# Batch 1 of a fused block-sparse attention and Swish MLP kernel: x transposes by DMA, odd value rows by ScalarE, pair 3's key maxima at another time, one copy for the last half tile, and a table load at another place

## The chip, the cores and the metric

The kernel runs on one core of a Trainium2 chip. The time is the device time in microseconds of one execution; the kernel before was run three times. A profile of one further execution gives, for each instruction, when it started and ended and what it waited for.

Engine names as in the profile: PE is TensorE (matmuls; PEld are its weight loads), DVE is VectorE, ACT is ScalarE, POOL is GpSimd, SP is SyncE. DMAs are issued from the queues of SP, ACT and POOL.

## The reference

```python
# q, k, v: (4, 8, 768, 64); block 32, window 16
k_sum = k.reshape(B, H, nb, block, D).max(axis=3)
v_sum = v.reshape(B, H, nb, block, D).mean(axis=3)
scores_l = scale * q @ k^T,  kept where |i - j| < window
scores_s = scale * q @ k_sum^T + log(block)
a = softmax over [scores_l, scores_s];   out = a @ [v, v_sum]
x = out, heads joined: (3072, 512)
h = x @ w_in                             # w_in (512, 2048)
g = h * sigmoid(beta * h)
result = g @ w_out                       # (3072, 512) float32
```

## The kernel before

**Tiling.** Four batches go one after the other; within a batch the eight heads go in four pairs (pair 0 to 3), each pair 128 wide, and the 768 positions in six tiles of 128. Attention gives x of a pair with positions in the partitions (`x_nat`); the first matmul needs it the other way round, so each pair is transposed into one quarter of `xT`. The MLP then makes `h` from all four quarters (`h_group`, L488: matmuls with `ki` 0 to 3, one for each pair, then Silu on ScalarE into `h_sb`), and the output tiles from `h_sb` (`o_part`, L512: 16 matmuls to a tile of 128 positions, in four parts, a copy out of PSUM, a DMA). The reciprocal of beta is folded into `w_out`.

**Local scores.** A score block sets 64 queries against a key row of 96 window keys, with the 24 block maxima behind them. Queries 0 to 63 of a tile use the even rows (`kw[:, 0]`, `ve`), queries 64 to 127 the odd rows (`kw[:, 1]`, `vo`), which are the same data 64 positions on. For a batch after the first:

- `cross` (L300) turns k and q of a pair by DMA transposes from SP's queue; `prep_k` and `prep_q` do it on PE, for pairs 0 and 1 of batch 1.
- `top_k` (L291, one DVE reduce) or `max_k` takes the block maxima; `rows_k` (L315, two DVE copies, L319 and L320) writes odd rows and maxima into `kw`.
- `copy_v` (L322) copies the odd rows `vo` from `ve`, two pieces to a pair, by DMA from SP's queue unless another way is handed in; `mean_v` and `rows_v` (L349, two DVE copies) add the block means behind each row, in `ve` and in `vo`.
- `scores` (L427) makes the scores of one half on PE and takes Exp on ScalarE; `mask` (L440) multiplies by the band on DVE; `av` (L444) multiplies with `ve` and `vo` on PE; `norm` (L459) divides on DVE into `x_nat`; `x_transpose` (L468) turns it: by six PE transposes with an identity and a DVE copy (L479, L480) in batches 0 and 1, by one DMA transpose on SP's queue (L474) in batches 2 and 3.

**PSUM.** A ring `big` of three buffers holds scores, av, `px` and h; a ring `t` of two holds the output tiles, so output tile n waits until tile n - 2 is copied out.

**Order.** Each engine runs its instructions in the order in which the program gives them; nothing is reordered. The main loop (L629 on) builds that order for one batch from two lists. `main` holds the batch's own h groups (1.3 apart on a nominal clock) and then its output parts (0.865 apart); the outputs start at `up` = 20.8. `side` holds the attention of the next batch, each call with a due time; before each main item all side calls that are due are issued. For batch 1, which is prepared in batch 0's time:

```python
first, step = up + 0.3, 4.4
t = first + step * g                              # scores and masks of pair g
p = (up - 9.0, up - 4.5, up + 7.5, up + 11.0)[g]  # maxima and rows_k
at_time(up + 5.8, copy_v, 1, g, 0, nch, nc.scalar.dma_start)   # pairs 2 and 3
m = up + 1.0 if g == 0 else first + step + 3.8    # means, rows_v
at_time(a + 2.9, x_transpose, (1, g), 0, nch, "big", dve)      # a = t + 3.5
```

The first two h groups of the next batch, with `ki` 0 to 2, come at the very end of a batch (unit 2 is batch 1's). Loads of q, k, v and weights are issued from POOL's queue; batch 2's start when a small memset (`open_gate`, L711) has run on DVE. Outputs go out on SP's queue, in order with the transposes and copies there. The last output tile is made in two halves of 256 columns (L530 on): DVE copies partitions 0 to 63 and SP sends them, ACT copies 64 to 127 and sends them.

ACT's function tables are loaded when the function changes: Silu's for the first time ahead of the first h group (L507), after the four transposes' copies of batch 0's first half (`x0`).

Of the kernel before, what the change touches and what calls it, by code (L numbers as in the profile page):

```python
# [12 lines left out]
def kernel(  # L13
# [10 lines left out]
    nc = tc.nc  # L24
    ctx.enter_context(tc.manual_schedule(engines={getattr(mybir.EngineType, e) for e in ("SP", "Pool", "PE", "DVE", "Activation")}))
    P = 128
    f32 = mybir.dt.float32
    bf16 = mybir.dt.bfloat16
    ALU = mybir.AluOpType
    ACTF = mybir.ActivationFunctionType  # L30

    B, H, S, D = q.shape
# [4 lines left out]
    nch = S // P  # L37
# [3 lines left out]
    npair = H // 2  # L41
# [17 lines left out]
    const = ctx.enter_context(tc.tile_pool(name="consts", bufs=1))  # L59
# [83 lines left out]
    A_avg = const.tile([P, NC, 32], bf16, name="A_avg")  # L143
    A_loc = const.tile([P, P // block + 1], bf16, name="A_loc")
    warm = const.tile([P, 512], bf16, name="warm")
    gate = const.tile([1, 16], f32, name="gate")
    near = const.tile([P, QT], bf16, name="near")
    band = const.tile([P, 2, nch, 2, QT], bf16, name="band")
# [59 lines left out]
    for t in km_bufs:  # L208
# [5 lines left out]
                         func=ACTF.Copy, scale=-NEG, bias=NEG)  # L214
# [45 lines left out]
    def psum(shape, dt, name, tag):  # L260
        if tag == "t":
            return ps.tile(shape, dt, name=name, tag="t", bufs=2)
        t = ps.tile([P, 2, 512] if dt == f32 else [P, 2, 1024], dt, name=name, tag="big", bufs=3)
        n = math.prod(shape[1:])
        flat = t[:, 0, 0:n]
        if len(shape) == 2:
            return flat
        return flat.rearrange("p (a b) -> p a b", b=shape[2])
# [199 lines left out]
    def x_transpose(key, m0, n, tag, copy):  # L468
        b, g = key[:2]
        if b not in xT:  # L470
            xT[b] = xt_pool.tile([P, k1, S], bf16, name="xT", tag="xT")
        x = x_nat.pop(key)
        if b > 1:
            nc.sync.dma_start_transpose(out=xT[b][:, g, :].rearrange("p (c f) -> p c f", f=P),  # L474
                                        in_=x.rearrange("p c h d -> p (c h d)"))
            return
        px = psum([P, n * P], bf16, "px", tag)
        for c in range(n):
            nc.tensor.transpose(px[:, c * P:(c + 1) * P], x[:, c].rearrange("p h d -> p (h d)"), identity)  # L479
        copy(out=xT[b][:, g, m0 * P:(m0 + n) * P], in_=px[:])  # L480
# [7 lines left out]
    def h_group(u, i, ks=range(k1)):  # L488

        b, t0, w = units[u]  # L490
        nn = 2 // w
        if 0 in ks:
            if (i * nn) % (k2 // w) == 0:
                h_bufs[(u, i * nn * w // k2)] = moe_pool.tile([P, k2 // w, w * MG], bf16, name="h_sb", tag="h_sb", bufs=4)
            h_open[(u, i)] = ps.tile([P, 2, 512], f32, name="h_ps", tag="big", bufs=3)
        big = h_open[(u, i)]
        for j in range(2):
            ni, tok = (i, t0 + j * MG) if w == 2 else (2 * i + j, t0)
            for ki in ks:
                nc.tensor.matmul(big[:, j, 0:MG], w_in_sb[:, ki, ni * P:(ni + 1) * P], xT[b][:, ki, tok:tok + MG],  # L500
                                 start=(ki == 0), stop=(ki == k1 - 1))
        if k1 - 1 not in ks:
            return
        for j in range(nn):
            ni = i * nn + j
            hb = h_bufs[(u, ni * w // k2)][:, ni % (k2 // w)]
            nc.scalar.activation(out=hb.rearrange("p (k m) -> p k m", m=MG), in_=big[:, j:j + w, 0:MG],  # L507
                                 func=ACTF.Silu, scale=beta_sb[:, ni:ni + 1])
# [3 lines left out]
    def o_part(u, ms, part, nparts):  # L512
        b, t0, w = units[u]
        row = b * nch + t0 // P + ms
        if part == 0:
            o_state["ps"] = ps.tile([P, d_model], f32, name="o_ps", tag="t", bufs=2)
            o_state["sb"] = moe_pool.tile([P, d_model], f32, name="o_sb", tag="o_sb", bufs=3)
        o_ps, o_sb = o_state["ps"], o_state["sb"]

        def dots(ni, c0, c1, o_ps=o_ps):  # L520
            nc.tensor.matmul(o_ps[:, c0:c1], h_bufs[(u, ni * w // k2)][:, ni % (k2 // w), ms * P:(ms + 1) * P],  # L521
                             w_out_sb[:, ni, c0:c1], start=(ni == 0), stop=(ni == k2 - 1))

        if u + 1 == len(units) and ms == w * HM - 1:

            c0, c1 = (part // 2) * (d_model // 2), (part // 2 + 1) * (d_model // 2)
            n = k2 // (nparts // 2)
            if part == nparts // 2:
                o_state["ps"] = o_ps = ps.tile([P, d_model], f32, name="o_ps", tag="t", bufs=2)
            for ni in range((part % 2) * n, (part % 2 + 1) * n):  # L530
                dots(ni, c0, c1, o_ps)
            if part % 2 == 1:
                for lo, hi, copy, eng in ((0, D, nc.vector.tensor_copy, nc.sync), (D, P, nc.scalar.copy, nc.scalar)):
                    copy(out=o_sb[lo:hi, c0:c1], in_=o_ps[lo:hi, c0:c1])  # L534
                    eng.dma_start(out=out_r[row, lo:hi, c0:c1], in_=o_sb[lo:hi, c0:c1])
            return
        n = k2 // nparts
        for ni in range(part * n, (part + 1) * n):
            dots(ni, 0, d_model)
        if part == nparts - 1:  # L540
            (nc.scalar.copy if u + 1 < len(units) else nc.vector.tensor_copy)(out=o_sb[:], in_=o_ps[:])  # L541
            nc.sync.dma_start(out=out_r[row], in_=o_sb[:])
# [3 lines left out]
    dve, act = nc.vector.tensor_copy, nc.scalar.copy  # L546
# [6 lines left out]
    def x0(g, copy):  # L553
        x_transpose((0, g, 0), 0, HM, "t", copy)
# [64 lines left out]
    x0(2, act)  # L619
    h_group(0, 1, range(2))  # L620
    x0(3, act)
    for i in range(2):
        h_group(0, i, range(2, 3))
    band_edge(True)
# [4 lines left out]
    for b in range(B):  # L629
        us = [u for u, z in enumerate(units) if z[0] == b]  # L630
        up = sum(NG[u] for u in us) * GT
# [5 lines left out]
        def at_time(t, f, *a):  # L637
            side.append((t, lambda: f(*a)))
# [13 lines left out]
        if nxt == 1:  # L652
            first, step = up + 0.3, 4.4
            for g in pairs:
                t = first + step * g
                p = (up - 9.0, up - 4.5, up + 7.5, up + 11.0)[g]
                if g < 2:
                    at_time(p, prep_k, 1, g, "t")
                    at_time(p + 0.8, prep_q, 1, g, "t", dve)
                    at_time(p + 0.8, copy_v, 1, g)  # L660
                else:
                    at_time(up + 0.5, cross, 1, g)
                    at_time(up + 5.8, copy_v, 1, g, 0, nch, nc.scalar.dma_start)
                at_time(p, top_k, 1, g)
                at_time(p, rows_k, 1, g)
                for par in range(2):
                    at_time(t, scores, 1, g, par)
                    at_time(t, mask, 1, g, par)
                if g % 2 == 0:
                    m = up + 1.0 if g == 0 else first + step + 3.8  # L670
                    at_time(m, mean_v, 1, (g, g + 1), "big")
                    for i in (g, g + 1):
                        at_time(m, rows_v, 1, i)
                a = t + 3.5
                at_time(a, av, (1, g), 0, nch)
                at_time(a, norm, (1, g), nch)
                at_time(a + 2.9, x_transpose, (1, g), 0, nch, "big", dve)
        elif nxt is not None:
            for g in pairs:
                t = (0.65, 1.95, 5.85, 9.75)[g]  # L680
                at_time(0.1, copy_v, nxt, g)
                at_time(t, cross, nxt, g)
                m = 3.9 + 3.9 * g if g < 3 else up + 2.0
                at_time(m, max_k, nxt, g)
                at_time(m, rows_k, nxt, g)
            at_time(10.0, mean_v, nxt, pairs)
            for g in pairs:
                at_time(10.1 + 1.0 * g, rows_v, nxt, g)
            for g in range(npair + 1):
                t = up + 4.0 * g  # L690
                if g < npair:
                    for par in range(2):
                        at_time(t, scores, nxt, g, par)
                        at_time(t, mask, nxt, g, par)
                if g:
                    at_time(t, av, (nxt, g - 1), 0, nch)
                    at_time(t, norm, (nxt, g - 1), nch)
                    at_time(t, x_transpose, (nxt, g - 1), 0, nch, "big", dve)
# [26 lines left out]
        for j, u in enumerate(us):  # L725
            n = units[u][2] * HM
            main += [(up + (4 * (j * n + ms) + p) * OT, lambda u=u, ms=ms, p=p: o_part(u, ms, p, 4)) for ms in range(n) for p in range(4)]
# [39 lines left out]
```

## Time and profile before

| | |
|---|---|
| median of 3 runs | 219.15 us (217.74, 219.15, 219.69) |
| profiled execution: its own time | 218.62 us |
| its span, first to last instruction | 216.9 us |
| PE matmul, busy | 207.0 us (95%) |
| PE weight loads, busy | 116.1 us (54%) |
| DVE, busy | 92.2 us (43%) |
| ACT, busy | 115.3 us (53%) |
| POOL, busy | 65.4 us (30%) |
| DMA | 28.25 MB, mean 130 GB/s |
| matmuls for h (L500) and output (L521) | 86.3 us and 83.9 us |

The times in the profile count from the span's start. Batch 0's attention fills the first 24 us with the loads of the weights; then h of batch 0 runs to about 48 us, its outputs, with batch 1's attention between them, to 78 us; batches 1, 2 and 3 follow, with h from 78, 125 and 171 us. A group is named by line, engine, operation and `out<-in` tiles; matmuls are pipelined, so the durations of single ones overlap. "idle before" and "waited for" name the releaser that came last.

### The profile page before, as it was taken

To read this page: it belongs to the slowest core of one execution; us is meant where nothing else is said; L and a number is where in the kernel's file an instruction comes from. 1 tells how busy PE (TensorE), PEld (TensorE's weight loads), DVE (VectorE), ACT (ScalarE), POOL (GpSimd) and SP (SyncE) were. 2 spreads that over 40 slices of the span, in tenths; PEclk is the share of its full clock that TensorE was granted. 3 is DMA by queue.
4 is the path that set the end of the run, shared out by engine and by line. 5 is a ranking of instruction groups with operands and counts; after the bars stand their busy time and mean duration, and the time that the engine had idled before them with its cause. 6 is when DMAs were issued, how large, how long until landed. Compare 5 with 4: busy or idle time off the path is not lost.

```text
span 216.9 us, 4971 instructions
## 1 busy us (share of the span) xinstructions
PE 207.0 (95%) x2064; PEld 116.1 (54%) x2082; DVE 92.2 (43%) x236; ACT 115.3 (53%) x162; POOL 65.4 (30%) x88
## 2 busy tenths in 40 slices
PE   7999999999997999999999999999999999999992
PEld 2656556564453556555555455555554556654461
DVE  3768763597769510654844202634455000002120
ACT  3796678777243147578443187668351476740001
POOL 7964244442099880696620000000000000000000
PEclk9999999999999999999999999999999999999999
DMA  7999999999999999999995646930334400001222
GB/s 177 183 150 195 205 206 207 183 174 165 191 142 190 184 205 197 149 156 141 155 167 127 165 125 134 124 73 4 96 75 133 131 6 0 0 0 51 97 86 59
DMA packets 91510, 28.25 MB, mean 130 GB/s; under 512 B 80720, under 2 KB 88160, under 8 KB 91488
## 3 DMA queue, kind: packets, MB, share of 16 engines
q0 software_dynamic: 62544, 13.24, 72.7%
q1 hardware_dynamic: 28304, 13.87, 30.2%
q10 hardware_dynamic: 640, 0.82, 1.4%
q8 instruction: 16, 0.26, 0.5%
q14 instruction: 6, 0.05, 0.1%
HBM read 27.27 MB, written 6.29 MB: 155 GB/s over the span
## 4 chain that ended last, share of the span: by engine, by line
PE 65%; DMA 21%; POOL 6%; DVE 2%; issue 2%; ACTq 1%; ACT 0%; POOLq 0%
PE o_ps L521 32%; PE h_ps L500 29%; DMA w_out_sb<-in_moe_w_out_dram 8%; DMA w_in_sb<-in_moe_w_in_dram 7%; DMA ve<-in_v_dram 4%; PE av_ps L455 2%; DMA vo<-ve 2%; PE s_ps L437 2%; POOL ve L118 1%; POOL w_in_sb L247 1%; POOL q_run L106 1%; POOL k_run L106 1%; ACTq L328 1%; PE vm_ps L340 0%; DVE attn L442 0%
## 5 line engine op out<-in xcount | busy, mean ns | idle before, releaser
L500 PE MATMUL h_ps<-xT,w_in_sb 128*128 128x384 bf16 x512 | 86.3, 326 | 0.3 <-ACT h_sb L507 0.3
L521 PE MATMUL o_ps<-w_out_sb,h_sb 128*128 128x512 bf16 (+1 forms) x383 | 83.9, 370 | 2.2 <-issue 1.9
L507 ACT ACTIVATE h_sb<-h_ps,beta_sb 128x768 bf16<-128x768 f32 (+1 forms) x80 | 59.2, 774 | 23.1 <-PE h_ps L500 22.9
L500 PEld LDWEIGHTS <-w_in_sb 128*128 128x128 bf16 x512 | 49.1, 98 | 32.6 <-issue 0.6
L521 PEld LDWEIGHTS <-h_sb 128*128 128x128 bf16 x400 | 37.4, 98 | 39.6
L541 ACT COPY o_sb<-o_ps 128x512 f32<-128x512 f32 x18 | 10.6, 587 | 37.4 <-PE o_ps L521 16.9
L442 DVE TENSOR_TENSOR attn<-attn,band 128x768 bf16<-128x768 bf16 x24 | 13.2, 557 | 24.0 <-ACT attn L438 22.6
L438 ACT ACTIVATE attn<-s_ps 128x768 bf16<-128x768 f32 x24 | 18.1, 808 | 8.9 <-PE s_ps L437 8.9
L111 POOL DMA_DIRECT2D k_nat<-in_k_dram x20 | 16.9, 856 | 13.9 <-DMA kw<-k_nat 7.5
L541 DVE COPY o_sb<-o_ps 128x512 f32<-128x512 f32 x5 | 3.5, 691 | 38.5 <-PE o_ps L521 38.5
L111 POOL DMA_DIRECT2D q_nat<-in_q_dram x20 | 16.5, 836 | 8.2 <-DMA w_out_sb<-in_moe_w_out_dram 4.5
L465 DVE TENSOR_TENSOR x_nat<-av_ps,r 128x768 bf16<-128x768 f32 (+1 forms) x20 | 15.9, 797 | 0.7
L118 POOL DMA_DIRECT2D ve<-in_v_dram x12 | 14.5, 1210 | 3.9 <-DMA w_in_sb<-in_moe_w_in_dram 2.7
L311 DVE TENSOR_TENSOR half<-kw 128x384 bf16<-128x384 bf16 x8 | 2.8, 356 | 25.4 <-DMA kw<-k_nat 25.4
L534 ACT COPY o_sb<-o_ps 64x256 f32<-64x256 f32 x2 | 0.7, 368 | 19.9 <-DVE o_sb L534 19.9
L293 DVE TENSOR_REDUCE km<-kw 128x24 bf16<-128x768 bf16 x8 | 7.6, 948 | 5.0 <-ACT kw L289 4.8
L455 PEld LDWEIGHTS <-attn 128*64 128x64 bf16 x336 | 6.8, 111 | 4.7 <-issue 2.3
L455 PE MATMUL av_ps<-ve,attn 128*64 128x65 bf16 x168 | 8.6, 198 | 0.5 <-DVE attn L442 0.4
L455 PE MATMUL av_ps<-vo,attn 128*64 128x65 bf16 x168 | 8.3, 197 | 0.3 <-DVE attn L442 0.3
L464 DVE RECIPROCAL r<-av_ps 128x12 f32<-128x12 f32 (+1 forms) x20 | 4.3, 214 | 9.9 <-PE av_ps L455 9.0
L437 PEld LDWEIGHTS <-kw 64*128 64x128 bf16 x288 | 4.9, 95 | 5.8 <-issue 4.4
L437 PE MATMUL s_ps<-qt,kw 64*128 64x64 bf16 x288 | 6.5, 191 | 0.8 <-DVE kw L320 0.6
(90 smaller groups left out, 148.0 us busy)
## 6 DMA issues: line engine op xcount, KB each, us to landing
out_dram<-o_sb SPq DMA_DIRECT2D x23, 256.0 KB, 2.3
w_out_sb<-in_moe_w_out_dram POOLq DMA_DIRECT2D x4, 512.0 KB, 17.1
k_nat<-in_k_dram POOLq DMA_DIRECT2D x20, 96.0 KB, 6.9
q_nat<-in_q_dram POOLq DMA_DIRECT2D x20, 96.0 KB, 6.3
w_in_sb<-in_moe_w_in_dram POOLq DMA_DIRECT2D x3, 512.0 KB, 14.4
ve<-in_v_dram POOLq DMA_DIRECT2D x6, 192.0 KB, 7.6
vo<-ve SPq DMA_DIRECT2D x10, 97.5 KB, 4.6
ve<-in_v_dram POOLq DMA_DIRECT2D x2, 384.0 KB, 13.1
```

The lines of the kernel that those rows point to most:

```text
L111: nc.gpsimd.dma_start(out=t[:, :, h], in_=(k_row if nm == "k" else q_row)[b, g, :, h])
L118: nc.gpsimd.dma_start(out=ve_bufs[b % 2][:, lo:hi, 0:D], in_=src)
L293: nc.vector.tensor_reduce(out=km_of[g], in_=keys_of(b, g).rearrange("p (n f) -> p n f", f=block), op=ALU.max, axis=mybir.AxisListType.X)
L437: nc.tensor.matmul(sv[:, h, m], kw[lo:lo + D, par, m, :], q[lo:lo + D, m, par], start=True, stop=True)
L438: nc.scalar.activation(out=a.rearrange("p m h f -> p h m f"), in_=sv, func=ACTF.Exp, scale=scale)
L442: nc.vector.tensor_mul(out=a, in0=a, in1=band[:, par])
L455: nc.tensor.matmul(ov[par * QT:(par + 1) * QT, h, m], a[:, par, m, h], t[:, PC * g + nch * h + m0 + m], start=True, stop=True)
L465: nc.vector.tensor_mul(out=x.rearrange("p m h d -> p h m d"), in0=ov[:, :, :, 0:D], in1=r[:, :, :, None].to_broadcast([P, 2, n, D]))
L500: nc.tensor.matmul(big[:, j, 0:MG], w_in_sb[:, ki, ni * P:(ni + 1) * P], xT[b][:, ki, tok:tok + MG], start=(ki == 0), stop=(ki == k1 - 1))
L507: nc.scalar.activation(out=hb.rearrange("p (k m) -> p k m", m=MG), in_=big[:, j:j + w, 0:MG], func=ACTF.Silu, scale=beta_sb[:, ni:ni + 1])
L521: nc.tensor.matmul(o_ps[:, c0:c1], h_bufs[(u, ni * w // k2)][:, ni % (k2 // w), ms * P:(ms + 1) * P], w_out_sb[:, ni, c0:c1], start=(ni == ...
L541: (nc.scalar.copy if u + 1 < len(units) else nc.vector.tensor_copy)(out=o_sb[:], in_=o_ps[:])
```

## The change

Five edits; the last of the short list below is a matter of due times only.

- `x_transpose` of batch 1: pairs 0 to 2 take the DMA transpose on SP's queue; pair 3 stays on PE and DVE.
- `copy_v` of batch 1, pairs 2 and 3: four copies on ACT in place of four DMAs from ACT's queue, at the same due time.
- A one-column Silu into a new tile `spare`, after the last of batch 0's first-half transposes, so that Silu's table is loaded there.
- The last output tile: DVE copies all 128 partitions of a half in one instruction; two DMAs, from SP and ACT, send it as before.
- Pair 3's maxima and `rows_k` of batch 1 are due at `up + 8.6` in place of `up + 11.0`; pair 3's `rows_v` at `first + 8.9` in place of `first + 8.2`, which puts it behind pair 2's masks.

In the order that results, DVE does pair 3's maxima and `rows_k` ahead of pair 2's masks, and pair 3's `rows_v` behind them. SP's queue holds, after batch 1's `cross`: output tiles 0 and 1, x of pair 0, tile 2, x of pair 1, tile 3, x of pair 2, tiles 4 and 5, then batch 2's `copy_v`. PE issues 18 transposes fewer; nothing else on PE or POOL changes its order.

```diff
+    spare = const.tile([P, 1], f32, name="spare")
...
-        if b > 1:
+        if b > 1 or (b == 1 and g < npair - 1):
             nc.sync.dma_start_transpose(out=xT[b][:, g, :].rearrange("p (c f) -> p c f", f=P),
                                         in_=x.rearrange("p c h d -> p (c h d)"))
...
-                for lo, hi, copy, eng in ((0, D, nc.vector.tensor_copy, nc.sync), (D, P, nc.scalar.copy, nc.scalar)):
-                    copy(out=o_sb[lo:hi, c0:c1], in_=o_ps[lo:hi, c0:c1])
+                nc.vector.tensor_copy(out=o_sb[:, c0:c1], in_=o_ps[:, c0:c1])
+                for lo, hi, eng in ((0, D, nc.sync), (D, P, nc.scalar)):
                     eng.dma_start(out=out_r[row, lo:hi, c0:c1], in_=o_sb[lo:hi, c0:c1])
...
     x0(3, act)
+    nc.scalar.activation(out=spare[:], in_=warm[:, 0:1], func=ACTF.Silu)
...
-                p = (up - 9.0, up - 4.5, up + 7.5, up + 11.0)[g]
+                p = (up - 9.0, up - 4.5, up + 7.5, up + 8.6)[g]
...
-                    at_time(up + 5.8, copy_v, 1, g, 0, nch, nc.scalar.dma_start)
+                    at_time(up + 5.8, copy_v, 1, g, 0, nch, act)
...
-                        at_time(m, rows_v, 1, i)
+                        at_time(m if i < 3 else first + step * 2 + 0.1, rows_v, 1, i)
```

## The prediction

> **What bounds the kernel now.** I read the page's busy table and slices first, then what PE waited for, then the chain that ended last, the timeline of the stretch it points at, and last the DMA landings.
>
> ```profile
> PE 207.0 (95%) x2064; PEld 116.1 (54%) x2082; DVE 92.2 (43%) x236; ACT 115.3 (53%) x162; POOL 65.4 (30%) x88
> ```
>
> PE is busy for 95% of the span, so only two things can move the time: work taken off PE, and gaps in it.
>
> ```profile
> PE av_ps L455 <- DVE attn L442: 0.6, 2, 0.4
> PE s_ps L437 <- DVE kw L320: 0.6, 1, 0.6
> PE h_ps L500 <- ACT h_sb L507: 0.3, 1, 0.3
> ```
>
> These are PE's longest waits on other engines once work has begun. All but the third lie in one place, as PE's busy time in that stretch shows (columns: stretch, its length, PE busy and instructions, clock, DMA share, GB/s).
>
> ```profile
> 65.94:69.92 3.98, 2.38 (x52) 1.00 2.12 191
> ```
>
> At full granted clock throughout, PE works 2.38 us in 4. The chain (start, duration, what) says who held it:
>
> ```profile
> 47.79 9.46 DMA ve<-in_v_dram
> ...
> 60.49 4.06 DMA vo<-ve
> ...
> 65.88 1.03 DVE attn L442 x2
> ```
>
> Batch 1's v of pairs 2 and 3 lands late, the odd rows vo are copied from it by DMA until 64.55, DVE stands in rows_v of pair 3 until then, and pair 2's masks and pair 3's maxima, queued behind on DVE, come too late for PE.
>
> **The change, part by part.**
>
> *PE transposes of pairs 0 to 2.* Three blocks of six matmuls go, with three DVE copies of 0.56 us that nothing but PE's buffers waited for.
>
> ```profile
> 71.83 0.34 PE px L479 x6
> 72.16 1.73 PE o_ps L521 x8
> ```
>
> PE's steady step is 0.216 us per output matmul, and a px block holds the chain 0.34: 3 x 0.34 = **1.02 us** gained. Pair 3 stays on PE.
>
> *The gap.* Three rows of PE's timeline:
>
> ```profile
> 64.21 1.89 PE L521 MATMUL o_ps<-w_out_sb,h_sb 128*128 128x512 bf16 x8
> 67.46 0.55 PEld L521 LDWEIGHTS <-h_sb 128*128 128x128 bf16 x4
> 69.92 1.41 PEld L521 LDWEIGHTS <-h_sb 128*128 128x128 bf16 x8
> ```
>
> Eight matmuls from 64.21 take 1.73 and 0.1 of turnover, so av of pair 2 could start at 66.04 and, with its 0.50, end at 66.54; it ended at 67.46: 0.92 lost. Four outputs need 0.96, so pair 3's scores could start at 68.42 and, with 0.46, end at 68.88; they ended at 69.92: 1.04 lost. Together **1.96 us**, if nothing new fills it. That rests on three edits at once.
>
> Odd rows by ScalarE: four DMAs go from ScalarE's queue, and four copies of 780 elements take their place in its stream, behind the same v load.
>
> ```profile
> 58.70 3.05 ACTq L328 DMA_DIRECT2D vo<-ve  x4
> 61.79 0.59 ACT L541 COPY o_sb<-o_ps 128x512 f32<-128x512 f32 x1 [4.54 <-DMA vo<-ve]
> 62.28 1.52 ACT L438 ACTIVATE attn<-s_ps 128x768 bf16<-128x768 f32 x2
> ```
>
> ```profile
> L289 ACT COPY kw<-pk 128x768 bf16<-128x768 bf16 x6 | 4.8, 800 | 1.7 <-PE pk L276 1.7
> L220 ACT COPY band<-near 128x384 bf16<-128x384 bf16 x4 | 1.8, 511 | 0.0
> ```
>
> The trace has no such copy. From below 768 elements at 0.80 us (from PSUM), from above twice the 384-element copy, 1.02; I take 0.81, as length decides and 768 is nearly 780. So 58.65 + 3.25 = 61.9 for the last, 2.6 us sooner than the DMA's landing. Queued behind on ScalarE: the copy of output tile 1 (to 62.5; before, 62.4) and pair 2's exponentials (to 64.0; before, 63.8). PE's tile 3 reuses tile 1's PSUM buffer: four matmuls after pair 2's scores, at 62.6 (before 63.0, less one px block), or 62.35 with the table term below. So ScalarE bounds PE at 62.55: a wait of 0 to 0.2; with 1.02 per copy, 1.0.
>
> Maxima of pair 3 sooner: reduce 0.95, rows_k 0.54, now ahead of pair 2's masks; pair 3's rows_v moves behind those masks. DVE's new stream: x of pair 1 until 61.2 (61.58 before, less one px block), means 61.5, rows_v of pair 2 62.2, maxima and rows_k 63.75, masks 64.8; PE wants them at 65.3. Uncertain is whether DVE's copies run as quickly as they can:
>
> ```profile
> 62.24 0.35 DVE L353 COPY vo<-vm 32x780 bf16<-32x780 bf16 x1
> 64.87 0.99 DVE L353 COPY vo<-vm 32x780 bf16<-32x780 bf16 x1
> 66.83 0.94 DVE L293 TENSOR_REDUCE km<-kw 128x24 bf16<-128x768 bf16 x1
> 67.69 0.57 DVE L319 COPY kw<-kw 128x576 bf16<-128x576 bf16 x1
> 68.30 0.71 DVE L320 COPY kw<-km 128x288 bf16<-128x288 bf16 x1
> ```
>
> The same copy took 0.35 or 0.99 while GpSimd issued loads, and pair 3's rows_k copies 0.57 and 0.71, where pair 2's, at 59.9, took 0.54 together. If both stretch again, the masks end at 65.55, a wait of 0.25. I put 0.1 in the sum, 0 to 0.4 in the range. [...]
>
> *Silu's table ahead.*
>
> ```profile
> 24.76 1.28 ACT L507 ACT_TABLE_LOAD   x1 [0.62 <-PE h_ps L500]
> 27.16 1.46 PE L500 MATMUL h_ps<-xT,w_in_sb 128*128 128x384 bf16 x8 [0.27 <-ACT h_sb L507]
> ```
>
> The load moves into ScalarE's 0.62 of idle; the one-column activation behind it costs less than the 0.51 of a 384-column copy; I take 0.2, so Silu starts about 0.4 sooner and PE's 0.27 goes. But the v landing at 58.65 doesn't move, and ScalarE's bound at 62.55 takes back 0.2. Worth **0.1**; 0 to 0.27.
>
> *One copy for the last half tile.*
>
> ```profile
> 212.90 0.42 DVE L534 COPY o_sb<-o_ps 64x256 f32<-64x256 f32 x1 [1.33 <-PE o_ps L521]
> 213.35 0.37 ACT L534 COPY o_sb<-o_ps 64x256 f32<-64x256 f32 x1 [1.34 <-DVE o_sb L534]
> 213.75 0.49 ACTq L535 DMA_DIRECT2D out_dram<-o_sb  x1
> ```
>
> ScalarE's half starts only after VectorE's ends. One 128x256 copy has the same 256 elements per partition, 0.42, and ScalarE's DMA then issues at 213.35: **0.40** gained, all of it at the end of the span; from below 0, if a 128-partition copy took the sum of both.
>
> *The DMA transposes, the new cost.* SP now carries output tile 1, x0, tile 2, x1, tile 3, x2, tiles 4 and 5, then batch 2's vo copies. Each transpose holds SP 1.2 to 1.7 us, so behind x2 the outputs of tiles 4 and 5 slip by that little, which nothing waits for. x2 needs pair 2's x (67.2, 1.4 behind the end of its av at 65.8, as before) and, before it in the queue, tile 3: copied at 68.58 to 69.17 before, 1.6 sooner now (two px blocks and 0.92), so out at 67.6 and x2 issued at 68.2. The first group of batch 1's h now starts at 78.12 - 1.02 - 1.96 - 0.1 + 0.1 = 75.14, and its third matmul reads pair 2, at 75.5. So x2 must land within 7.3 us. The DMA views of short stretches give us from issue to landing (last column): for the transposes issued at 108.2, at 121.7, for the two pairs between 48.1 and 53.4, and for those at 93.3 and 95.0:
>
> ```profile
> xT<-x_nat SPq DMA_TRANSPOSE x1, 6.2
> xT<-x_nat SPq DMA_TRANSPOSE x1, 2.7
> kw<-k_nat SPq DMA_TRANSPOSE x2, 7.5
> qt<-q_nat SPq DMA_TRANSPOSE x2, 8.6
> kw<-k_nat SPq DMA_TRANSPOSE x1, 8.5
> qt<-q_nat SPq DMA_TRANSPOSE x1, 10.4
> ```
>
> ```profile
> 66.00:72.00 6.00, 4.40 (x66) 2.48 (x67) 5.56 (x10) 2.10 (x3) 5.59 (x7) 1.00 2.18 178
> 104.00:110.00 6.00, 5.84 (x76) 2.94 (x77) 3.56 (x9) 2.50 (x4) 3.84 (x5) 1.00 2.36 175
> ```
>
> 2.7 is a queue without loads. From 66 to 72 batch 2's loads run (DMA share 2.18), as they did beside the 6.2 (2.36), and x2 has two transposes and two outputs close ahead, as the 7.5 and 8.6 had. I take 8.0: x2 lands at 76.2, PE waits **0.7**; between 6.2 (nothing) and 10.4 (3.1). x0 and x1, issued near 63.0 and 65.2 behind tiles 1 and 2 (copied by 62.5 and 64.6), land before 75.
>
> [...]
>
> Behind this stage everything follows PE. Batch 2's first scores have their keys ready long before:
>
> ```profile
> 88.32 0.36 DVE L311 TENSOR_TENSOR half<-kw 128x384 bf16<-128x384 bf16 x1 [9.11 <-DMA kw<-k_nat]
> 99.65 0.52 PE L437 MATMUL s_ps<-qt,kw 64*128 64x64 bf16 x24
> ```
>
> Those keys, landed at 88.3, need 1.7 us on DVE, so 9 us of cover against a PE 3 us earlier and loads delayed by a transpose or two.
>
> **Sum**: -1.02 - 1.96 - 0.1 - 0.4 + 0.1 + 0.7 = -2.7 us on the profiled execution (218.62 us for its span of 216.9): 215.9. That execution lies 0.5 below the median of the runs, 219.15; against the mean of it and the three runs, 218.8, it gives **216.1**.
>
> **Rivals.**
> 1. *The x transpose takes the gap's place.* x2 lands 9.5 to 10.4 after issue, PE waits 2.2 to 3.1 ahead of h: 218.8 - 3.4 + 2.65 = 218.1. For it: 8.6 and 10.4 above, in a loaded queue. Against it: 6.2 at the higher share.
> 2. *Slower: SP's queue is served one entry at a time.* Batch 2's last keys and queries landed at 93.3 + 8.5 and 95.0 + 10.4, 3.6 apart. If all five entries from x0 to x2 need 3.6 each from 63.0 on, x2 lands at 81.0 and PE waits 5.5: 218.8 - 3.4 + 5.5 = 220.9. It decides from a landing at 78.9 on, where the 3.4 is spent. Against it: the four transposes issued 1.8 us apart from 48.1 on landed 7.5 and 8.6 later, so the queue kept pace with them.
> 3. *The change does not do what it says:* ScalarE's copies at 1.02 and stretched DVE copies keep a gap of 1.0 + 0.4 where 1.96 was: 218.8 - 3.4 + 1.3 + 0.7 = 217.4. For it: 0.99 above. Against it: three of four such copies were quick.
>
> **How the numbers follow.** Forecast 0.57 (its own range 215.0 to 217.0), rival 1 0.20, rival 2 0.13, rival 3 0.10. A measurement here tells about 1% from no change, 2.2 us. Faster by more: the forecast and a part of rival 3, 0.60; within: rival 1, the rest of 3 and half of rival 2, 0.29; slower by over 1%: the worse part of rival 2, 0.11. The range goes from no wait and no lost table term (218.8 - 3.7, and 0.9 for the spread of runs), 214.2, to rival 1 with its wait at 10.4, 219.0.
>
> **What would show it.** Right: no px in batch 1 but pair 3's; DVE no longer waits for DMA vo<-ve; ScalarE's four copies end near 61.9; pair 2's av starts within 0.4 of the outputs ahead of it; h starts near 75.1 and waits under 1.5 for a transpose; the last output DMA issues 0.4 after DVE's copy starts. Wrong: a wait above 2 us in h for xT, ScalarE's copies above 1 us, or batch 2's scores waiting for keys.

## The result and the profile after

The changed kernel takes 221.02 us (median of 20, 218.31 to 223.52), the kernel before 217.45 us (median of 20): ratio **1.0115, 95% interval 1.0082 to 1.0147**, slower by about 1%. The ratio leaves out executions more than 1.5% above the fastest of their kernel, here four of the changed kernel's; the two medians are 1.6% apart. I had forecast 216.1 with a range to 219.0.

Its times fall apart by the clock that the profiler recorded for TensorE: 4 executions at 0.999 or 1.0 (median 218.8), 16 at 0.985 to 0.992 (median 221.3). The profiled one, 218.48 for a span of 216.8, is one of the four; a profile of a usual one follows in the experiments.

The page of the profiled execution: the head, and the row of the costliest group, whose last part is idle time ahead of the group and what ended it.

```profile
span 216.8 us, 4938 instructions
PE 205.6 (95%) x2046; PEld 114.5 (53%) x2064; DVE 90.7 (42%) x233; ACT 118.0 (54%) x165; POOL 65.7 (30%) x88
...
L501 PE MATMUL h_ps<-xT,w_in_sb 128*128 128x384 bf16 x512 | 86.6, 326 | 2.8 <-DMA xT<-x_nat 2.8
```

TensorE is busy 1.4 us less (207.0 before), and a new idle entry stands beside h. The waits of TensorE on DMA and other engines behind the first weights (total, times, longest):

```profile
PE h_ps L501 <- DMA xT<-x_nat: 2.8, 2, 2.6
PE o_ps L522 <- ACT o_sb L542: 0.2, 1, 0.2
```

The waits on DVE's attn and kw are gone, and so is the one on the first Silu. The timeline of the stage (start, duration, what, idle before it):

```profile
58.37 3.42 ACT L329 COPY vo<-ve 64x780 bf16<-64x780 bf16 x4 [1.67 <-DMA ve<-in_v_dram]
...
62.45 2.75 PE L522 MATMUL o_ps<-w_out_sb,h_sb 128*128 128x512 bf16 x12 [0.15 <-ACT o_sb L542]
...
68.59 1.49 SPq L475 DMA_TRANSPOSE xT<-x_nat  x1
...
74.91 0.33 PE L501 MATMUL h_ps<-xT,w_in_sb 128*128 128x384 bf16 x1
75.43 0.32 PE L501 MATMUL h_ps<-xT,w_in_sb 128*128 128x384 bf16 x1 [0.19 <-DMA xT<-x_nat]
78.37 5.85 PE L501 MATMUL h_ps<-xT,w_in_sb 128*128 128x384 bf16 x35 [2.61 <-DMA xT<-x_nat]
```

The stage runs almost to the tenth as forecast: ScalarE's copies end at 61.8 (61.9), the output restarts at 62.45 (62.55), h starts at 74.91 (75.14; 78.12 before). Then the third matmul waits for pair 2's x until 78.37, and by then everything gained against the profile of before is spent. In the chain of waits (start, length, what) this transpose stands with its landing, 9.73 after issue; the times from issue to landing of the two ahead of it are in the DMA view of short stretches:

```profile
68.59 9.73 DMA xT<-x_nat
78.37 10.23 PE h_ps L501 x62
```

```profile
xT<-x_nat SPq DMA_TRANSPOSE x1, 6.4
xT<-x_nat SPq DMA_TRANSPOSE x1, 10.4
```

This explains 218.5, but neither 221.0 nor why before's median is 217.4 where its profile was 218.6.

### The profile page after: what moved, and what is told of

The parts are those of the page before. It is cut to its first block, busy times and chain, and to the rows that moved or that the text cites. A ratio compares the mean times of both kernels' runs of the same rounds, so it can differ in the third digit from the quotient of the medians.

```text
span 216.8 us, 4938 instructions
## 1 busy us (share of the span) xinstructions
PE 205.6 (95%) x2046; PEld 114.5 (53%) x2064; DVE 90.7 (42%) x233; ACT 118.0 (54%) x165; POOL 65.7 (30%) x88
## 4 chain that ended last, share of the span: by engine, by line
PE 64%; DMA 24%; POOL 6%; ACT 2%; issue 2%; DVE 0%; ACTq 0%; POOLq 0%
PE o_ps L522 31%; PE h_ps L501 29%; DMA w_out_sb<-in_moe_w_out_dram 8%; DMA w_in_sb<-in_moe_w_in_dram 7%; DMA ve<-in_v_dram 5%; DMA xT<-x_nat 4%; PE av_ps L456 2%; PE s_ps L438 2%; ACT vo L329 2%; POOL ve L118 1%; POOL w_in_sb L248 1%; POOL q_run L106 1%; POOL k_run L106 1%; PE vm_ps L341 0%; POOL q_nat L111 0%
## 5 line engine op out<-in xcount | busy, mean ns | idle before, releaser
L439 ACT ACTIVATE attn<-s_ps 128x768 bf16<-128x768 f32 x24 | 18.2, 809 | 8.6 <-PE s_ps L438 8.6
L400 ACT ACTIVATE attn<-s_ps 128x768 bf16<-128x768 f32 x8 | 6.2, 809 | 0.9 <-PE s_ps L384 0.7
L552 PE MATMUL w_ps<-warm 128*128 128x512 bf16 x13 | 5.2, 570 | 1.3 <-DVE warm L156 1.3
```

The costliest lines, as they stand in the source:

```text
L439: nc.scalar.activation(out=a.rearrange("p m h f -> p h m f"), in_=sv, func=ACTF.Exp, scale=scale)
```

## The experiments

Two theories at the start. **A**: the late transposes are the whole loss, by the wait and by what the wait does to the clock. **B**: the clock or the time is lost by the other edits. All ratios are to the kernel before, with a 95% interval.

**The changed kernel with x on TensorE again (e1).**

```
-        if b > 1 or (b == 1 and g < npair - 1):
+        if b > 1:
```

> The changed kernel with batch 1's x of pairs 0 to 2 transposed by TensorE again; the other four edits stay. Theory A (the late transposes are the whole loss: TensorE stands 2.8 us for the third, and that gap also costs it the clock of 0.992 that most executions of the changed kernel show): no wait for xT in h, 1.0 us more of TensorE transposes, 216.3 to 217 on a profile and a clock as before's; about 1.3% faster than the kernel before. Theory B (the other edits cost the clock or the time): still slower than before, clock 0.992 in most executions.

Measured: 216.77, ratio 0.9968 (0.9941 to 0.9995); the clock 0.997 or more in all 12 executions. So the transposes do make the loss, of time and of clock. But the gain is 0.3%, not 1.3%. The timeline has part of the reason:

```profile
59.94 3.42 ACT L329 COPY vo<-ve 64x780 bf16<-64x780 bf16 x4 [2.89 <-DMA ve<-in_v_dram]
63.38 0.58 ACT L542 COPY o_sb<-o_ps 128x512 f32<-128x512 f32 x1
...
64.01 1.02 PE L522 MATMUL o_ps<-w_out_sb,h_sb 128*128 128x512 bf16 x4 [1.04 <-ACT o_sb L542]
```

In this execution v landed 1.6 later than in the changed kernel's profile, and ScalarE, holding the four copies in order ahead of the output's copy, passed 1.04 of it on to TensorE.

**The transposes alone, on the kernel before (e2).**

```
-        if b > 1:
+        if b > 1 or (b == 1 and g < npair - 1):
```

> The kernel before with the DMA transposes of batch 1's x alone; none of the other edits. Theory A: output tile 3 leaves later here than in the changed kernel, the third transpose is issued near 70 and lands near 79, h would start near 77.1, so a wait of 2 us or more in h and a clock of 0.992 as in the changed kernel; 220.5 to 223, slower than before by 1 to 2%. Theory B: about as before, clock as before.

Measured: 219.53, ratio 1.0101 (1.0068 to 1.0135), under the 220.5 to 223 expected: only five executions of 12 ran at 0.992 (median 221.4), seven at 0.998 or more (219.2). The profile is of one of the five; the timeline, and short windows (TensorE's busy time first, then the granted clock as third number from the end):

```profile
80.18 4.16 PE L500 MATMUL h_ps<-xT,w_in_sb 128*128 128x384 bf16 x15 [2.42 <-DMA xT<-x_nat]
```

```profile
79.00:80.00 1.00, 0.00 (x0) 0.00 (x0) 0.00 (x0) 0.07 (x1) 0.21 (x1) 1.00 1.72 194
80.00:81.00 1.00, 0.82 (x6) 0.49 (x6) 0.00 (x0) 0.00 (x0) 0.50 (x1) 1.00 1.81 226
81.00:82.00 1.00, 1.00 (x5) 0.49 (x4) 0.00 (x0) 0.00 (x0) 0.36 (x1) 0.52 2.39 152
```

TensorE stands 2.42 us, and 0.9 us after it resumes, at 80.18, its granted clock falls to one half (0.52 from 81 to 82, 0.50 from 82 to 84).

**The changed kernel once more (e6)**, unedited, to find this in it.

> The changed kernel, once more, for a profile of its usual execution (16 of 20 at a clock of 0.992). Theory A: the wait for the third transpose is there, 2.5 us or more, and behind it h runs for about 3 us at half clock, 1.7 us lost, as in the kernel before with the transposes alone; about 221. Rival: the loss of clock lies elsewhere in the span, away from the gap.

Measured: 220.71, clock 0.992. The chain of waits, and windows of 1 us:

```profile
68.97 9.89 DMA xT<-x_nat
78.90 11.92 PE h_ps L501 x62
```

```profile
79.00:80.00 1.00, 1.00 (x7) 0.51 (x7) 0.00 (x0) 0.00 (x0) 0.60 (x2) 0.88 2.42 156
80.00:81.00 1.00, 1.00 (x5) 0.48 (x4) 0.00 (x0) 0.00 (x0) 0.79 (x1) 0.50 2.26 197
81.00:82.00 1.00, 1.00 (x5) 0.48 (x4) 0.00 (x0) 0.00 (x0) 0.54 (x1) 0.50 1.24 313
82.00:83.00 1.00, 1.00 (x5) 0.48 (x4) 0.00 (x0) 0.86 (x2) 0.28 (x1) 0.50 1.71 240
83.00:84.00 1.00, 1.00 (x8) 0.50 (x7) 0.00 (x0) 0.83 (x2) 0.10 (x1) 0.91 2.23 170
```

The wait is the same (2.8), but behind it the clock stands at one half for 0.24 + 3 + 0.18 = 3.4 us (from the shares 0.88 and 0.91), and the 62 matmuls of h take 11.92 instead of 10.23: 1.7 us. The rest of the span runs at 1.0. Of the 2.5 us between the two groups of executions 1.7 is this; the other 0.8 I did not take apart.

The traces also show in what an execution that loses the clock differs from one with the same gap that does not. The stretches in their record of the clock agree with whole numbers of 3.413 us: 3.41 at half in e6, 3.4 in e2 and in e8, 6.8 in e7 (two), and 211.63 at full in the changed kernel's first profile, up to the fall behind the last work (62). Counted in such windows from the changes of the clock, e6's gap lies inside one window, in which TensorE is busy for 0.87 us, and the next window runs at half. In the changed kernel's first profile the gap lies across two, busy for 1.81 and 2.21, and neither is followed by half clock (e6's rows first, then those of the changed kernel's first profile; columns as above):

```profile
76.35:79.77 3.42, 0.87 (x6) 0.54 (x6) 0.10 (x1) 0.83 (x1) 1.59 (x2) 1.00 1.72 189
79.77:83.18 3.41, 3.41 (x13) 1.51 (x11) 0.00 (x0) 1.04 (x2) 1.67 (x2) 0.50 1.77 243
```

```profile
73.75:77.17 3.42, 1.81 (x13) 0.88 (x12) 0.66 (x2) 1.87 (x2) 1.87 (x2) 1.00 1.66 189
77.17:80.58 3.41, 2.21 (x14) 1.36 (x14) 0.00 (x0) 0.07 (x1) 1.39 (x2) 1.00 1.96 211
```

Over all thirteen profiles the same count divides cleanly: each full-clock window with 1.41 us or less of TensorE work (e2 1.00, e8 1.22, e4 1.41 at its end) was followed by half clock, and none with 1.59 or more (at their ends e8 1.59, e7 1.73). So in these profiles the clock fell where 2.0 us or more of a window of 3.41 were idle, and stayed where 1.8 or less were. As an estimate from these numbers, a gap of 2.8 escapes at a quarter to a third of the positions; 4 of 20 executions did.

**Work in the gap (e4).** Twelve matmuls on spare data ahead of the first that reads pair 2's x:

```
+                if u == 2 and i == 0 and j == 0 and ki == 2:
+                    w_ps = ps.tile([P, 512], f32, name="w_ps", tag="t", bufs=2)
+                    for _ in range(12):
+                        nc.tensor.matmul(w_ps[:], warm[:, 0:P], warm, start=True, stop=True)
```

> The changed kernel with 12 matmuls of 512 columns on spare data ahead of the first h matmul that reads pair 2's x: TensorE works through the wait, the wait itself stays. Nothing of the result changes. Theory A, its part on the clock: the landing near 78.3 still sets h's third matmul, so a profile of 218.3 to 219, but the clock comes back to 0.999 in most executions and the median falls from 221.0 to about 218.5 to 219. Theory B (the clock does not hang on this gap): the median stays at 221, clock 0.992.

Measured: 219.41 (218.5 to 219 expected), ratio 1.0078 (1.0048 to 1.0108), and the clock 0.995 or more in all 12. The timeline:

```profile
76.59 0.32 PE L505 MATMUL h_ps<-xT,w_in_sb 128*128 128x384 bf16 x1 [0.46 <-DMA xT<-x_nat]
76.75 2.75 PE L504 MATMUL w_ps<-warm 128*128 128x512 bf16 x12
79.45 4.71 PE L505 MATMUL h_ps<-xT,w_in_sb 128*128 128x384 bf16 x28
```

The useful work resumes no sooner than in e6, yet 1.6 us of the median come back with the clock. Here idleness, not the wait as such, cost the clock: 0.995 or more in all 12 with the spare matmuls, 0.992 or less in 16 of 20 without them.

**Pair 2 on TensorE, pairs 0 and 1 by DMA (e3).**

```
-        if b > 1 or (b == 1 and g < npair - 1):
+        if b > 1 or (b == 1 and g < npair - 2):
```

> The changed kernel with pairs 0 and 1 by DMA transposes and pair 2 by TensorE. Theory A: the second transpose, issued near 65, lands by 75 to 75.5, h wants it at its second matmul near 75.6: a wait under 0.5 us and a clock near 1.0; 216 to 217, faster than before by 1 to 1.5%. Theory B: like the changed kernel, near 221. A third outcome (SP's queue serves entries one at a time): with the third transpose gone, the second lands clearly sooner than 10.4 us after issue.

Measured: 217.04, ratio 0.9970 (0.9938 to 1.0002), clock 0.995 or more in all; TensorE waits for no xT. As A has it on wait and clock, but again 0.3% and not the 1 to 1.5% expected. The second transpose landed 10.1 after its issue, no sooner than beside the third.

**Why they land late.** A1: batch 2's loads share the DMA engines. A2: SP's queue serves its entries, 256 KB outputs among them, one after the other. **Loads later (e7)** and **outputs from ScalarE's queue (e8):**

```
-                    at_time(up + 7.0, open_gate)
+                    at_time(up + 16.0, open_gate)
...
-                    at_time(up + 7.1 + 0.1 * g if b == 0 else 1.0 + 4.5 * g, load_next, nxt + 1, g)
+                    at_time(up + 16.1 + 0.1 * g if b == 0 else 1.0 + 4.5 * g, load_next, nxt + 1, g)
```

```
-            nc.sync.dma_start(out=out_r[row], in_=o_sb[:])
+            (nc.scalar if b == 0 else nc.sync).dma_start(out=out_r[row], in_=o_sb[:])
```

> The changed kernel with the gate of batch 2's loads 9 steps later in the written order, near 70 instead of 57.4, so that GpSimd issues none of them while x of pairs 0 to 2 is transposed. Theory A1 (the transposes land late because batch 2's loads share the DMA engines): the third lands within 5 us of its issue, no wait in h, 216 to 217, unless batch 2's keys then come late near 100. Theory A2 (they land late because SP's queue serves its entries, the 256 KB outputs among them, one after the other): landing still 8 to 10 us, the wait stays, about 221.

> The changed kernel with the outputs of batch 0 issued by ScalarE's queue instead of SP's (eight issues of about 0.5 us on ScalarE, off the path at most places). Theory A1 (shared DMA engines, batch 2's loads): the transposes land 8 to 10 us after issue as before, though issued up to 1 us sooner; wait 2 us or more. Theory A2 (SP's queue in order, outputs ahead of each transpose): they land 3 to 6 us after issue, the wait goes, near 216.5.

Measured: e7 225.88, ratio 1.0371 (1.0301 to 1.0440); e8 222.80, ratio 1.0246 (1.0186 to 1.0307). Both lose, in places of their own, but both answer. In e7 the three transposes land 2.7, 4.5 and 3.2 after issue, at a third of the DMA share (second number from the end of a window's row; e7's first, the changed kernel's below it):

```profile
xT<-x_nat SPq DMA_TRANSPOSE x1, 2.7
xT<-x_nat SPq DMA_TRANSPOSE x1, 4.5
xT<-x_nat SPq DMA_TRANSPOSE x1, 3.2
```

```profile
66.00:72.00 6.00, 5.84 (x71) 2.94 (x71) 3.62 (x9) 2.55 (x5) 0.10 (x1) 1.00 0.71 182
```

```profile
66.00:72.00 6.00, 5.84 (x71) 2.85 (x71) 2.79 (x5) 2.59 (x4) 4.96 (x7) 1.00 2.14 157
```

h does not wait for x at all. In e8, with SP's queue free of outputs and the loads as they were, they land after 5.6, 5.0 and 8.4, between the two forecasts; the first two are issued 4 to 6 us sooner than in the changed kernel, so only the third (67.4 instead of 68.6) compares. So the loads carry most: without them the third needs 3.2 instead of 9.7, without the outputs ahead of it 8.4. Whether they delay it by sharing the DMA engines, as A1 says, or in another way, e7 does not tell. What e7 and e8 lost:

```profile
PE vm_ps L341 <- DMA ve<-in_v_dram: 5.8, 2, 4.8
```

```profile
ACT L508 <- DMA out_dram<-o_sb: 5.5, 1, 5.5
```

In e7 batch 2's v is now late for TensorE, and the clock falls behind that gap as well (0.50 from 93.0 to 99.8). In e8 ScalarE's first Silu stands behind an output's issue that itself waits for the output before it to land; TensorE waits 3.75 for ScalarE.

**The kernel before once more (e5)**, unedited, for what the other edits had to gain.

> The kernel before, once more, for a second profile: its executions lie in two groups, near 217 and near 219, and the profile that the prediction used (218.62) is of the upper one. If the size of the gap ahead of pair 2's av and batch 1's h varies with the landing of v, an execution near 217 shows the same waits as before but a batch 1 h that starts about 1.5 us sooner (near 76.7 to 77). If the groups come from the clock, it shows the same starts and another clock.

Measured: 217.54, clock 0.999. The waits of TensorE and the timeline:

```profile
PE av_ps L455 <- DVE ve L353: 0.3, 1, 0.3
PE h_ps L500 <- ACT h_sb L507: 0.3, 1, 0.3
```

```profile
58.76 2.64 ACTq L328 DMA_DIRECT2D vo<-ve  x4
...
63.10 0.35 DVE L353 COPY vo<-vm 32x780 bf16<-32x780 bf16 x1
63.47 0.57 DVE L353 COPY ve<-vm 32x780 bf16<-32x780 bf16 x1
...
76.69 0.50 PE L479 MATMUL px<-identity,x_nat 128*128 128x128 bf16 x6
77.03 3.25 PE L500 MATMUL h_ps<-xT,w_in_sb 128*128 128x384 bf16 x19
```

The gap at 66 to 70 is not there: the odd rows land before VectorE asks for them (63.45), and h starts at 77.03 instead of 78.12, though this execution was 0.9 behind the other at 60 (pair 1's av at 60.6 instead of 59.7). The 1.96 us was a property of the profiled execution, not of a usual one. It is not unique: e2's profile, with the same odd-row DMAs, stands 1.6 us for the masks of pair 2.

**The odd rows and the sooner maxima alone (e9).** On the kernel before:

```
-                p = (up - 9.0, up - 4.5, up + 7.5, up + 11.0)[g]
+                p = (up - 9.0, up - 4.5, up + 7.5, up + 8.6)[g]
...
-                    at_time(up + 5.8, copy_v, 1, g, 0, nch, nc.scalar.dma_start)
+                    at_time(up + 5.8, copy_v, 1, g, 0, nch, act)
...
-                        at_time(m, rows_v, 1, i)
+                        at_time(m if i < 3 else first + step * 2 + 0.1, rows_v, 1, i)
```

> The kernel before with ScalarE's copies of the odd rows and the sooner maxima of pair 3 alone. The prediction priced this at 1.96 us. Theory C (the 1.96 us of gap is of the one execution that was profiled; an execution of 217.5 stands 0.3 us there): 0 to 0.3 us gained in the median, ratio 0.997 to 1.001. Theory D (the gap is there in most executions): 1.5 to 2 us gained, ratio 0.991 to 0.993.

Measured: 217.06, ratio 0.9998 (0.9980 to 1.0016). Theory C stands: the edit is worth nothing that 12 executions can show. Its profile has pair 1's av at the same 60.6 as e5's and starts h at the same 77.03:

```profile
77.03 3.25 PE L500 MATMUL h_ps<-xT,w_in_sb 128*128 128x384 bf16 x19
```

**Hiding the landing.** In the first two groups of batch 1's h, pair 2 comes last (**e10**); and each transpose is also issued right behind the normalisation that writes its x (**e11**). For e10, with the same exchange of 2 and 3 in the last index of a group:

```
-            main += [(total + i, lambda i=i: h_group(us[-1] + 1, i, range(k1 - 1))) for i in range(2)]
+            for n, ks in enumerate(((0, 1), (3,)) if nxt == 1 else (range(k1 - 1),)):
+                main += [(total + 2 * n + i, lambda i=i, ks=ks: h_group(us[-1] + 1, i, ks)) for i in range(2)]
```

and for e11 on top of it:

```
-                at_time(a + 2.9, x_transpose, (1, g), 0, nch, "big", dve)
+                at_time(a + (2.9 if g == npair - 1 else 0.0), x_transpose, (1, g), 0, nch, "big", dve)
```

> The changed kernel with another order of the contraction in the first two groups of batch 1's h: pairs 0 and 1 for both groups, then pair 3, then pair 2, so TensorE has 12 matmuls (12 x 0.163 us, 10.40 us for 64) instead of 2 ahead of the first that reads pair 2's x. The third transpose still lands near 78.3. Theory A: the wait falls from 2.6 to 2.8 us to 1.0 to 1.4, and a gap that short costs no clock: clock 0.996 or more in most executions, near 217.0, ratio about 0.998. If any gap of over 1 us costs the clock: clock 0.992 still in most executions, near 219.

> The same order of the contraction, and each DMA transpose of batch 1's x issued right behind the normalisation that writes it, ahead of one 256 KB output more on SP's queue. x of pair 2 is written at 67.0 and was issued at 68.6. Theory A: issued near 67.0, it lands by 77 at 9.7 us from the issue, sooner if the outputs ahead of it cost it time; TensorE wants it near 76.9: a wait under 0.5 us, no loss of clock, and the 1.0 us of TensorE transposes saved: 215.5 to 216.3, ratio 0.991 to 0.996, faster than before and than the changed kernel with the transposes on TensorE. If the landing moves out with the earlier issue (the loads of batch 2 set it), the wait is as in the run with the order alone.

Measured: e10 218.20, ratio 1.0026 (0.9999 to 1.0053); e11 216.89, over the 215.5 to 216.3 expected, ratio 0.9975 (0.9946 to 1.0005). The clock is 0.996 or more in all 24 executions. e10's wait is where it was expected,

```profile
75.04 2.11 PE L501 MATMUL h_ps<-xT,w_in_sb 128*128 128x384 bf16 x12
78.19 2.11 PE L501 MATMUL h_ps<-xT,w_in_sb 128*128 128x384 bf16 x12 [1.04 <-DMA xT<-x_nat]
```

so a gap of 1 us cost no clock in any of them, but its median is 1.2 over what I expected; its executions spread from 216.4 to 219.3, the profiled one (217.2) lies low, and I did not find what the others add. In e11 the third transpose, issued at 67.81 with one output less ahead of it, lands after 7.7; the waits of TensorE:

```profile
xT<-x_nat SPq DMA_TRANSPOSE x1, 7.7
```

```profile
PE h_ps L501 <- DMA xT<-x_nat: 1.0, 2, 0.5
```

Of the kernels here, e1, e3 and e11 lie at 0.997; only e1's interval excludes no change. Moving the transposes to the DMA is worth nothing measurable even where nothing waits long for them.

## Why the prediction was wrong, step by step

- **The baseline and the gap (priced 1.96): failed.** I subtracted a gap found in one execution from a mean near that execution (218.8). By the three runs that I had, that execution lay low; in fact it lay high: of the 35 of the kernel before that ran beside e1 to e4, four lie above its 218.62, of the 20 beside the changed kernel six, and the medians are 217.41 and 217.45. A usual one has 0.3 of waits there (e5), and removing their cause gains nothing (e9). Three runs that spread over 2 us were too few to call the profiled one typical, and I asked only how to scale to the median, not whether the gap itself made the difference. On the profiled executions alone the sum ahead of h was right: h starts 3.2 us sooner, where 3.0 was forecast.
- **x2's landing (8.0 taken, 10.4 as bound): mis-sized.** 9.73 and 9.89 measured, issued at 68.6 to 69.0 rather than 68.2; the wait is 2.6 to 2.8, not 0.7. This is rival 1's mechanism at rival 1's price. The choice of 8.0 was between rows whose DMA share and queue I matched only by eye; e7 shows that batch 2's loads make most of it.
- **Rival 2, SP's queue one entry at a time:** not what happened. e7 keeps the queue, and the entries land after 2.7 to 4.5; e8 gives the outputs ahead of them a small part.
- **The clock: missing.** No term and no rival asked what a gap of TensorE costs beyond itself, though rivals 1 and 2 were made of such a gap. It costs 1.7 us in e6, and by their mean clock in 16 of 20 executions. With it, rival 1 would have been slower than before.
- **18 transposes less (1.02 on the path):** TensorE's busy time fell by 1.4. No run isolates the term.
- **ScalarE's copies: right in size** (0.81 taken, 0.84 to 0.85 measured), and so was the bound that they set at 62.55. What I did not price is that this bound moves with v's landing, and passes 1.04 on where v is late (e1).
- **VectorE's copies (0.1 in the sum, 0.25 if they stretch again):** pair 2's masks end at 64.61 (64.8 forecast), pair 3's rows_k copies take 0.49 and 0.23, and TensorE waits for no mask. The term was nothing.
- **Silu's table:** loaded ahead as forecast, and the 0.3 wait for the first Silu is gone. No run isolates it; two executions of the kernel before differ by 0.9 at 60 us, so 0.1 would not show.
- **Batch 2's cover of 9 us: enough.** Its transposes start later on SP (87.4 instead of 84.6) and VectorE has the first keys at 92.96 instead of 88.32, so about 5 us of the cover are left; its first scores still start without a wait, at 99.63.
- **The last copy (0.40): not found.** Issue and landing of the last two DMAs, in the DMA view, changed kernel:

```profile
out_dram<-o_sb SPq DMA_DIRECT2D x1, 64.0 KB, 1.9
out_dram<-o_sb ACTq DMA_DIRECT2D x1, 64.0 KB, 2.2
```

Both are issued at 213.3 and the later needs 2.2; before, ScalarE's was issued at 213.75 and needed 2.0. So 0.25 is gained to the landing. But from the end of TensorE's last matmul to the end of the span there are 4.0 us in both kernels, and 3.7 to 4.1 in the other profiles, with the old copy (e2, e5, e9) as with the new: at the end of the span no gain shows.

- **The arithmetic of the range and chances:** rival 1 with its wait of 3.1 gives 218.5 by its own terms, not 219.0. Rival 1, the rest of rival 3 and half of rival 2 make 0.335 for within and leave 0.065 for slower, not 0.29 and 0.11.

The sum, redone from a usual execution, with the wait as measured: 217.4 - 1.0 - 0.1 + 2.8 = 219.1. The four executions of the changed kernel at full clock lie at 218.3 to 219.3, their median at 218.8; the clock takes the other 16 to 221.3. That agrees, but a sum with a term fitted to the runs does not prove the small ones.

## What to carry to other kernels

Before a gap in a profile is counted as something to gain, see whether the profiled execution lies at the median of enough runs; if it lies above, the gap may be what makes it lie there. The third transpose by DMA landed 3.2 us after its issue with batch 2's loads away (e7, DMA share 0.71 from 66 to 72) and 9.7 beside them (changed kernel, 2.14), for the same 196 KB: take its price from rows with the load that it will meet, and set it against how soon after its issue it is wanted. A wait that left TensorE idle for 2.6 to 2.8 us cost 1.7 us more by the clock in e6 and nothing more in the changed kernel's first profile, depending on where it fell, so a move that takes work off TensorE must not open one.

## What the runs showed of the hardware

Behind an idle gap of 2.4 to 2.8 us on TensorE the granted clock stood at 0.50 for 3.4 us, starting 0.9 us after work resumed (e6, e2); the mean clock that goes with it, 0.992 or less, was that of 16 of 20 executions of the changed kernel and 5 of 12 of e2. In e7, behind a window without any TensorE work, it stayed at 0.50 for two windows, 6.8 us; TensorE worked for 2.4 us of the first of them. In the kernels whose profile shows gaps of about 1 us at most (e10, e11), or spare matmuls in the gap (e4), the mean clock was 0.995 or more in all 36 executions; the 0.995 and 0.997 in the profiles of e4 and e3 go with a fall behind the last matmul (0.97 and 0.91 from 200 to 217). Two executions of the kernel before, of the 71 beside the experiments, ran at 0.992 as well (218.65 and 222.19), and no profile shows why. DMA transposes of 128x768 landed 2.7 to 4.5 us after issue at a DMA share of 0.71 from 66 to 72 (e7), and 6.4 to 10.4 in the changed kernel, e2, e3, e4, e6 and e10, at a share of 1.7 to 1.8 between issue and landing in the changed kernel's first profile; with fewer outputs ahead of them in the queue they landed 4.3 to 8.4 after issue, at 1.4 to 2.4 from 60 to 78 (e8, e11).
